# A spectral kernel that also compares its DFT matrices: a smaller table for the comparison, turned on the chip for the second half, and another order of the steps

## The chip, the cores and the metric

The kernel runs on one core of a Trainium2 chip. The metric is device time in microseconds (us), the median of several runs. A profile is one more execution, recorded by the hardware profiler. The engines are TensorE (PE: matmuls, PEld: their weight loads), VectorE (DVE), ScalarE (ACT), GpSimd (POOL) and SyncE (SP). Each works through its own queue in order; semaphores tie them together. Transfers (DMA) are issued by SP and POOL and share 16 DMA engines.

## The reference

Two independent results stand side by side, 2048 rows by 512 columns each, in float32:

```python
# A: global filter
X = jnp.fft.rfft2(x); X = X * (w_r + 1j * w_i); y = jnp.fft.irfft2(X, s=(S, D))
# B: Fourier mixing with given matrices
a = einsum("bsd,ed->bse", x, dft_hid_re); b = einsum("bsd,ed->bse", x, dft_hid_im)
y = einsum("ts,bse->bte", dft_seq_re, a) - einsum("ts,bse->bte", dft_seq_im, b)
```

B's matrices are inputs: two of 2048 x 2048 (`dft_seq`, 16 MB each, called C or `cm` in the kernel) and two of 512 x 512 (`dft_hid`, 1 MB each, `wd`).

## The kernel before

Both halves are computed as fast transforms from tables that are part of the program. For B this is right only if the given matrices are the DFT matrices, so the kernel also loads all of C and `dft_hid` and compares every element with a table. If one differs, a flag is set and a general path (`_b_from_c`, a branch at the end) computes B from the matrices. With the usual inputs that branch is not taken.

**The order is written by hand.** Each piece of work is a named step (`@step`), and the string `PLAN` (line 23) lists all steps; each engine's queue takes its instructions in that order. The names:

- A forward: `xa` loads, `fold` (VectorE), `hid` (TensorE), `zs` (ScalarE), `f16_` (TensorE), `ys` (ScalarE), for eight blocks.
- A per slot n = 0 to 7 of the spectrum: `w` (load of the weights and, right behind, of the slot's table `fi`), `tr` (TensorE), `ez`, `tf` (ScalarE), `sf` (VectorE), `fwd` (TensorE), `wf` (ScalarE), `prod` and `comb` (VectorE, the product with the weights), `yf` (ScalarE), `inv` (TensorE), `ev` (ScalarE).
- A inverse: `hi` (TensorE), `eu` (ScalarE), `g16_` (TensorE), `sc` (ScalarE), `eo` (VectorE), `st` (store by POOL). `hi` and `g16_` use three banks of PSUM in turn with the other steps; `eo` frees a bank.
- B: `xb` loads, `xr` (ScalarE), `al` (TensorE), `av` (ScalarE), `bh` (TensorE), `hv` (ScalarE), `ro` (TensorE), `y1`, `y3` (ScalarE), `y2` (VectorE), `pt` (stores by POOL). `al`, `bh` and `ro` share two banks of PSUM, which `av`, `hv`, `y1` and `y2` free.
- The comparison: `cl` loads 1 MB of C or `dft_hid` into one of six blocks (`blk`, which `xa` and `xb` use too), `cc` compares it on VectorE (`unequal`, line 736: one scalar_tensor_tensor that multiplies by a small constant, compares and counts, in place), `tt` loads a table. `rs`, `pf` and `flag` add up the counts.

The rows of the DFT matrices are symmetric, so a table of 1024 rows by 513 columns, for the cosine and the sine, covers C. It is cut into four tables of 512 rows (`tt0`, `tt1` for the first half of the rows, `tt3`, `tt4` for the second), held in two buffers, and `dft_hid` has its own smaller table (`tt2`, called `hs`). A table serves a whole half of the columns after ScalarE has changed the sign of its odd columns (`sg`, line 754).

**Branch hints.** Twelve steps before the end of the plan (line 823) a hint of the branch at the end is given on PE, ACT and DVE.

Of the kernel before, what the change touches and what calls it, by code (L numbers as in the profile page):

```python
# [24 lines left out]
fold5 xb0 xb3 xb2 hid3 ys1 hid2 zs3 cc0 cl3 f16_3 zs2 cc1 cl4 f16_2 ys3 hid5 ys2 xb1 fold7 hid4 zs5 cl5 f16_5
zs4 cl6 cc2 hid6 ys5 w0 xb4 f16_4 hid7 cc3 ys4 zs6 zs7 f16_6 w1 cc4 xr0 f16_7 sg0 w2 cc5 al0 ys6 late ys7 al1
av0 tr0 cc6 av1 tr1 ez0 wf0 al2 ez1 sf0 al3 av2 sf1 tf0 wf1 fwd0 cl7 av3 xb7 tf1 xb6 xb5 tr2 prod0 xb8 wf2
xb10 fwd1 ez2 cl9 cl8 comb0 fwd2 xb11 cc7 yf0 xb9 xb12 inv0 g2 xr1 prod1 w3 sg1 al4 ev0 sx2 al5 w4 av4 tr3
comb1 av5 spec2 al6 ez3 al7 av6 sf3 yf1 tr4 cl11 av7 prod2 xr2 cl12 inv1 xb13 ez4 tf3 al8 xb15 wf3 comb2 ev1
al9 av8 xb14 wf4 fwd3 av9 sf4 yf2 spy cc8 al10 w5 tf4 al11 av10 cc9 tr5 av11 cl10 inv2 ez5 prod3 cl14 xr3 cl13  # L30
wf5 comb3 al12 w6 ev2 al13 av12 al14 cc10 av13 yf3 al15 av14 fwd4 sf5 cl15 av15 cc11 tf5 bh8 prod4 tt2 tr6 hv8
cl16 wf6 inv3 ez6 comb4 bh0 w7 ev3 sf6 fwd5 yf4 hv0 cc12 tf6 ro0 cc13 cl18 tr7 wf7 cl17 y10 fwd6 ez7 y20 prod5
y30 rx bh1 ry cc14 pt0 bh2 hv1 ro1 comb5 hv2 cl21 cl19 inv4 y11 y21 bh3 yf5 ev4 sf7 y31 prod6 ro2 tf7 pt1 hv3
fwd7 y12 y22 bh4 comb6 y32 pt2 inv5 hv4 cc15 yf6 ro3 ev5 inv6 cc16 y13 cl20 tt3 bh5 ev6 y23 cl22 sg2 prod7 ro4
y33 hv5 pt3 y14 bh6 y24 comb7 y34 ro5 hv6 pt4 bh7 y15 y25 yf7 cc17 y35 inv7 hv7 pt5 ro6 ev7 cc18 tt4 ro7 y16
hi0 cc19 cl23 cl24 y17 cc20 hi1 eu0 cc21 hi2 eu1 cc22 cl25 sg3 cl26 cl30 y27 cl27 g16_0 cc23 y37 pt7 g16_1 eu2
cc24 cl28 sc0 hi3 sc1 eo0 cl29 y26 cc25 y36 hi4 eu3 pt6 eo1 cl31 sg4 cc26 st0 g16_2 g16_3 cc27 eu4 cl32 sc2
hi5 sc3 eo2 eo3 cc28 st1 hi6 eu5 cc29 g16_4 cc30 g16_5 eu6 sc4 cc31 cl33 hi7 sc5 eo4 eo5 g16_6 eu7 cc32 st2
# [189 lines left out]
def kernel(  # L228
# [78 lines left out]
    wsp_sb = const("wsp_sb", 8, 2, 2, 2, src=wsp, by=pool)  # L307
    odd = const("odd", 2, src=tabs["odd"], by=pool)
    turn = sp.tile([P, 8], mybir.dt.int32, name="turn")
    pool.dma_start(turn, tabs["turn"])  # L310
# [288 lines left out]
    def _():
        load(fb, tabs["fb"].rearrange("p (k v n) -> p k v n", k=2, v=2))  # L600
# [138 lines left out]
    def compare(i, k, q, mt, half, tb):  # L739
        raw = "c", i  # L740

        def four(name):
            return at[name].rearrange("p (j c) -> p j c", j=4)

        @step(f"cl{i}")
        def _():
            lo = 4 * half + 2 * q
# [1 line left out]
            load(four(raw).rearrange("p (r j) c -> p r j c", r=2), cm[mt, tb, lo : lo + 2].rearrange("r p j c -> p r j c"))

        if half and tb == 0:
            @step(f"sg{k}")
            def _():
                act.mul(at["t", k][:, :, 1::2], at["t", k][:, :, 1::2], -1.0)
# [8 lines left out]
    def compare_hidden(i, h):
        def four():
            return at["c", i].rearrange("p (j c) -> p j c", j=4)

        @step(f"cl{i}")
        def _():
            block(("c", i))
            load(four().rearrange("p (m j) c -> p m j c", m=2),  # L770
                 wd[:, :, 2 * h : 2 * h + 2].rearrange("m p j c -> m p j c").rearrange("m p j c -> p m j c"))

        if h:
            @step("sg2")
            def _():
                for mt in range(2):
                    act.mul(at["hs"][:, :, mt, 1::2], at["hs"][:, :, mt, 1::2], -1.0)

        @step(f"cc{i}")
        def _():  # L780
            for mt in range(2):
# [4 lines left out]
    def table(k, q, mt):  # L786
        @step(f"tt{k}")
        def _():
            t = sp.tile([P, 4, 513], F32, name="tt", bufs=2)
            if q is None:  # L790
                at["hs"] = t.rearrange("p a b -> p (a b)")[:, :1028].rearrange("p (k m f) -> p k m f", k=2, m=2)
                load(at["hs"], tabs["hs"])
            else:
                at["t", k] = t
                load(t, tabs["tt"][mt, q])

    for k, (q, mt) in enumerate(((0, 0), (0, 1), (None, None), (1, 0), (1, 1))):
        table(k, q, mt)
        if q is None:
            for h in range(2):  # L800
                compare_hidden(16 + h, h)
        else:
            for j in range(8):
                half, tb = divmod(j, 4)
                compare(18 * q + 8 * half + 4 * mt + tb, k, q, mt, half, tb)
# [143 lines left out]
```

## Time and profile before

| What | Value |
|---|---|
| runs (3) | median 191.54 us, 190.98 to 191.56 |
| the profiled execution | 191.75 us, span 190.0 us |
| mean granted TensorE clock | 0.975 |
| loads and stores | 66.05 MB, 348 GB/s over the span |
| compares of C, 128x2048, with and without `odd` | 16 at 2349 ns, 16 at 2286 ns |

The span runs from the first to the last instruction; the rest of the execution's time lies around it. "Busy" adds up the instructions of an engine. Rows of the timeline give start, duration, engine, line, operation, written<-read, and in brackets the idle time before, with what ended it.

### The profile page before, as it was taken

How to read it: one execution, taken by the hardware profiler on the slowest of the kernel's cores; microseconds unless marked ns; L12 is line 12 of the kernel's file. 1: busy time of each engine (PE TensorE's matmuls, PEld its weight loads, DVE VectorE, ACT ScalarE, POOL GpSimd, SP SyncE). 2: the span in 40 equal slices, each digit the busy share in tenths (PEclk: the TensorE clock that was granted, in tenths of full speed). 3: DMA queues.
4: the chain of work that ended last, by engine and by line, in shares of the span. 5: the costliest groups of instructions: out<-in, count | busy, mean ns of one | idle time of the engine just before them, and what ended most of it. 6: DMA issues, size and time to landing. Idle time of an engine off the chain costs nothing.

```text
span 190.0 us, 2792 instructions
## 1 busy us (share of the span) xinstructions
PE 171.7 (90%) x1022; PEld 147.6 (78%) x1022; DVE 162.8 (86%) x217; ACT 88.3 (46%) x145; POOL 23.4 (12%) x32
## 2 busy tenths in 40 slices
...
GB/s 187 303 425 407 430 412 399 406 403 403 378 403 398 398 387 404 284 416 400 389 355 345 307 321 154 197 286 411 232 418 414 411 414 422 418 411 292 200 256 12
DMA packets 19668, 66.05 MB, mean 348 GB/s; under 512 B 1792, under 2 KB 2688, under 8 KB 18752
## 3 DMA queue, kind: packets, MB, share of 16 engines
...
q8 instruction: 10, 0.16, 0.3%
q14 instruction: 10, 0.08, 0.1%
...
## 4 chain that ended last, share of the span: by engine, by line
DMA 35%; PE 30%; DVE 25%; issue 4%; ACT 1%; SPq 1%; DVEq 0%
DMA blk<-in_cm 16%; DVE blk L737 15%; DMA blk<-in_xa 14%; PE pa L515 5%; DMA w<-in_wa 4%; PE pa L447 4%; PE pb L643 4%; PE pb L642 4%; DVE work L571 3%; PE pb L668 3%; PE pa L518 2%; PE pa L425 2%; PE pa L451 2%; PE pb L680 2%; PE pb L664 1%
## 5 line engine op out<-in xcount | busy, mean ns | idle before, releaser
L737 DVE SCALAR_TENSOR_TENSOR blk<-blk,tt 128x2048 f32<-128x2048 f32 (+2 forms) x24 | 41.3, 1752 | 2.6 <-DMA blk<-in_cm 2.6
L737 DVE SCALAR_TENSOR_TENSOR blk<-blk,odd,tt 128x2048 f32<-128x2048 f32 x16 | 37.4, 2349 | 6.7 <-DMA blk<-in_cm 6.6
L550 PE MATMUL pa<-ta,fz 128*128 128x256 f32 x128 | 29.6, 389 | 1.0 <-DVE work L571 1.0
L550 PEld LDWEIGHTS pa<-ta,fz 128*128 128x128 f32 x128 | 28.8, 305 | 1.7 <-issue 1.3
L555 ACT COPY work<-pa 128x1024 f32<-128x1024 f32 x8 | 8.1, 1013 | 22.9 <-PE pa L550 12.0
L485 DVE TENSOR_TENSOR work<-pa,w 128x1024 f32<-128x1024 f32 x14 | 16.4, 1216 | 1.1 <-PE pa L447 1.1
L383 ACT COPY fz<-pa 128x1024 f32<-128x1024 f32 x8 | 15.2, 1976 | 4.3 <-PE pa L379 4.3
L347 DVE TENSOR_TENSOR work<-blk 128x1024 f32<-128x1024 f32 (+1 forms) x10 | 10.1, 1009 | 7.0 <-DMA blk<-in_xa 7.0
L379 PE MATMUL pa<-square,work 128*128 128x128 f32 x128 | 15.3, 276 | 0.7 <-ACT work L372 0.7
L372 ACT COPY work<-pa 128x1024 f32<-128x1024 f32 x8 | 8.0, 1019 | 16.5 <-PE pa L368 16.5
L379 PEld LDWEIGHTS pa<-square,work 128*128 128x128 f32 x128 | 14.9, 194 | 0.9 <-ACT work L372 0.9
L562 PEld LDWEIGHTS pa<-square,work 128*128 128x128 f32 x128 | 14.8, 192 | 0.7 <-issue 0.6
L562 PE MATMUL pa<-square,work 128*128 128x128 f32 x128 | 15.0, 276 | 0.3 <-DVE work L571 0.3
L643 PE MATMUL pb<-fb,xr 128*128 128x200 f32 (+1 forms) x64 | 14.7, 311 | 0.0
L642 PE MATMUL pb<-fb,blk 128*128 128x200 f32 (+1 forms) x64 | 14.6, 310 | 0.0
L515 PEld LDWEIGHTS pa<-fi,work 128*128 128x128 f32 x112 | 13.4, 192 | 1.1 <-issue 1.0
L515 PE MATMUL pa<-fi,work 128*128 128x128 f32 x112 | 13.6, 275 | 0.0
L447 PE MATMUL pa<-work,fi 128*128 128x512 f32 x28 | 13.3, 596 | 0.1
L642 PEld LDWEIGHTS pb<-fb,blk 128*128 128x128 f32 x64 | 10.8, 190 | 0.5 <-issue 0.5
L643 PEld LDWEIGHTS pb<-fb,xr 128*128 128x128 f32 x64 | 10.7, 190 | 0.3 <-ACT xr L632 0.3
L367 PE MATMUL pa<-ta,work 128*128 128x256 f32 x32 | 10.6, 417 | 0.0
L522 ACT COPY fz<-pa 128x1024 f32<-128x1024 f32 x8 | 8.1, 1009 | 5.2 <-PE pa L515 5.2
...
## 6 DMA issues: line engine op xcount, KB each, us to landing
...
tt<-tab_tt SPq DMA_DIRECT2D x4, 1026.0 KB, 9.1
...
```

Source lines behind the costliest of these rows:

```text
L347: TT(out=us[:, h, own].rearrange("p c k f -> p c (k f)"), in0=xs(b)[:, own, 0], in1=xs(b)[:, own, 1], op=op)
L367: mm(even, v[:, 0, 1, r], hd0, start=True, stop=False)
L379: mm(y[:, r, c], zs[:, r, 128 * c : 128 * c + 128], f16, start=True, stop=True)
L383: act.copy(fz.rearrange("p c k (n g) -> p g (c k n)", g=16)[:, i::8], flat(at["py", i]))
L447: mm(flat(px[:, h]), ft[:, 0], flat(t[:, h]), start=True, stop=True)
L485: TT(out=m[:, h].rearrange("p i (r q) f -> p i r (q f)", r=2), in0=x2, in1=w2, op=MUL)
L515: mm(pi[:, i, q], lhs[i], it[:, 0], start=True, stop=True)
L550: mm(pu[:, k, h], gz[:, 2 * h + q, 2 * j + k], at["di"][:, h, q], start=q == 0, stop=q == 1)
L562: mm(po[:, k, q // 2, q % 2], u[:, k, q], f16, start=True, stop=True)
L642: mm(bank[:, lo : lo + w], x[:, g, k], fb[:, n // 15, 0, :w], start=True, stop=False)
L643: mm(bank[:, lo : lo + w], xr[:, g, k], fb[:, n // 15, 1, :w], start=False, stop=True)
L737: dve.scalar_tensor_tensor(raw, raw, k, v, op0=MUL, op1=ALU.not_equal, accum_out=stat[:, i : i + 1])
```

## The change

- **Tables.** Only 512 rows by 513 columns remain, for the cosine (`tt0`) and the sine (`tt1`), both held throughout. For rows 512 to 1023 the angle grows by a quarter turn per column: even columns keep their table up to sign, odd columns take the other table. ScalarE makes this exchange in place between the halves (`swa`, `swb`, with a temporary in a buffer of `yb`).
- **`dft_hid`** is compared with every fourth column of the same table, one matrix per load (before: half the rows of both matrices per load, with its own table).
- **Loads.** `fb`, `odd` and `turn` are one load (`mixed`); `wsp` moves from POOL's queue to SP's; `bt` is cut into `bt` and `bm`.
- **The order** of the plan is another one.
- **Hints.** PE and ACT keep theirs twelve steps before the end; DVE's now stands ahead of the last compare, and POOL and SP get one there too.

The diff, cut to its core:

```diff
 PLAN = """
-xa0 ta tt0 xa1 xa2 xa3 xa5 cl0 fb fold0 cl1 hid0 bt xa7 fold1 tt1 we hid1 zs0 cl2 fold3 f16_0 zs1 f16_1 ys0
+xa0 ta xa1 fb xa2 xa3 cl0 tt0 xa5 fold0 cl1 xa7 fold1 hid0 bm bt zs0 hid1 xb0 fold3 f16_0 zs1 wsp f16_1 ys0
...
-    th = _ang(np.outer(np.arange(S // 2), np.arange(513)), S)
-    tt = np.stack([np.cos(th), -np.sin(th)]).reshape(2, 2, 4, 128, 513).transpose(0, 1, 3, 2, 4)
+    th = _ang(np.outer(np.arange(512), np.arange(513)), S)
+    tt = np.stack([np.cos(th), -np.sin(th)]).reshape(2, 4, 128, 513).transpose(0, 2, 1, 3)
...
+    tt = [const(f"tt{mt}", 4, 513) for mt in range(2)]
...
         @step(f"cc{i}")
         def _():
-            for mt in range(2):
-                for n, (lo, hi, v, neg) in enumerate(((0, 257, at["hs"][:, :, mt], False),
-                                                      (257, 512, at["hs"][:, :, mt, 255:0:-1], mt == 1))):
-                    unequal(32 + 4 * h + 2 * mt + n, four()[:, 2 * mt : 2 * mt + 2, lo:hi], v, -TINY if neg else TINY)
+            t, neg = tt[mt], mt
+            for tb in range(4):
+                unequal(32 + 4 * mt + tb, four(i)[:, :, 128 * tb : 128 * tb + 128],
+                        t[:, :, 512:0:-4] if tb % 2 else t[:, :, 0:512:4],
+                        odd[:, neg * (tb % 2) : neg * (tb % 2) + 1] if tb in (1, 2) else (-TINY if neg * (tb % 2) else TINY))
...
+    @step("swa")
+    def _():
+        tmp = at["tmp"] = sp.tile([P, 2, 512], F32, name="yb", bufs=2).rearrange("p a (j c) -> p (a j) c", j=2)
+        act.copy(tmp, tt[0][:, :, 1::2])
+        act.copy(tt[0][:, :, 1::4], tt[1][:, :, 1::4])
+        act.mul(tt[0][:, :, 3::4], tt[1][:, :, 3::4], -1.0)
+        negate(tt[0][:, :, 2::4])
+
+    @step("swb")
+    def _():
+        act.mul(tt[1][:, :, 1::4], at["tmp"][:, :, 0::2], -1.0)
+        act.copy(tt[1][:, :, 3::4], at["tmp"][:, :, 1::2])
+        negate(tt[1][:, :, 2::4])
...
-    for at_step, name in enumerate(plan):
-        if at_step == len(plan) - 12:
+    last = [name for name in plan if name.startswith("cc")][-1]
+    for name in plan:
+        hinted = {plan[-12]: (pe, act), last: (dve, pool, sync)}.get(name)
+        if hinted:
             tc.no_sync_barrier()
-            tc.mark_branch_hint_location("general", hint="LikelyTaken", engines=[e.engine for e in (pe, act, dve)])
+            tc.mark_branch_hint_location("general", hint="LikelyTaken", engines=[e.engine for e in hinted])
```

What the other order is, at three places. First VectorE's queue where A's forward transform ends and the spectrum begins, before (L737 is a compare, L435 and L436 are `sf0` and `sf1`, L485 is `prod0`):

```order
L737 SCALAR_TENSOR_TENSOR blk,stat<-blk,odd,tt 128x2048
L737 SCALAR_TENSOR_TENSOR blk,stat<-blk,tt 128x2048 x2
L737 SCALAR_TENSOR_TENSOR blk,stat<-blk,odd,tt 128x2048 x2
L435 TENSOR_TENSOR work<-pa,work 128x2x256
L436 TENSOR_TENSOR work<-work,pa 128x2x256
L435 TENSOR_TENSOR work<-pa,work 128x2x256
L436 TENSOR_TENSOR work<-work,pa 128x2x256
L485 TENSOR_TENSOR work<-pa,w 128x1024 x2
```

And now (L744, L439, L440 and L489 are the same four):

```order
L744 SCALAR_TENSOR_TENSOR blk,stat<-blk,mixed,tt_105 128x2048
L744 SCALAR_TENSOR_TENSOR blk,stat<-blk,tt_105 128x2048
L744 SCALAR_TENSOR_TENSOR blk,stat<-blk,tt_106 128x2048
L744 SCALAR_TENSOR_TENSOR blk,stat<-blk,mixed,tt_106 128x2048
L439 TENSOR_TENSOR work<-pa,work 128x2x256
L440 TENSOR_TENSOR work<-work,pa 128x2x256
L439 TENSOR_TENSOR work<-pa,work 128x2x256
L440 TENSOR_TENSOR work<-work,pa 128x2x256
L744 SCALAR_TENSOR_TENSOR blk,stat<-blk,mixed,tt_106 128x2048
L489 TENSOR_TENSOR work<-pa,w 128x1024 x2
```

The last compare of this stage, `cc6`, has moved from ahead of `sf0` to behind `sf1`.

Second, ScalarE's queue in the middle of the kernel, where B's first rows come out, before (L429 is `ez`, L477 `wf`, L689 `y10`, L700 `y30`, L711 and L712 `ry`, L673 `hv`):

```order
L440 COPY work<-pa 128x4
L477 COPY w<-we 128x4
L689 COPY yb<-pb 128x2x257
L429 COPY work<-pa 128x512
L700 COPY yb<-yb 128x2x255
L711 COPY yb<-pb 1x257
L712 COPY yb<-yb 1x255
L673 COPY zb<-pb 128x512 x2
```

And now, from `ez6` (L433) on; L526 is `ev4`, L696 `y10`:

```order
L433 COPY work<-pa 128x512
L802 COPY yb<-tt_105 128x1024
L803 COPY tt_105<-tt_106 128x4x128
L804 ACTIVATE tt_105<-tt_106 128x4x128
L785 ACTIVATE tt_105<-tt_105 128x4x128
L526 COPY fz<-pa 128x2x4x128
L696 COPY yb<-pb 128x2x257
L481 COPY w<-we 128x4
```

The four instructions of `swa` (L802 to L785) now stand ahead of `ev4` and `y10`; the three of `swb` stand in the same way between `ry` and the next `hv`, `hv2`.

Third, the end of VectorE's queue, before (L571 is `eo`, L811 `rs`, L819 `flag`):

```order
L737 SCALAR_TENSOR_TENSOR blk,stat<-blk,odd,tt 128x2048
L942 BRANCH_PREFETCH_HINT
L571 TENSOR_TENSOR work<-pa,work 128x2x2x128 x4
L737 SCALAR_TENSOR_TENSOR blk,stat<-blk,tt 128x2048
L811 TENSOR_REDUCE rs<-stat 128x1
L819 TENSOR_SCALAR flag<-pb 128x1
```

And now:

```order
L744 SCALAR_TENSOR_TENSOR blk,stat<-blk,mixed,tt_106 128x2048
L575 TENSOR_TENSOR work<-pa,work 128x2x2x128 x4
L950 BRANCH_PREFETCH_HINT
L744 SCALAR_TENSOR_TENSOR blk,stat<-blk,tt_106 128x2048
L817 TENSOR_REDUCE rs<-stat 128x1
L825 TENSOR_SCALAR flag<-pb 128x1
```

The hint has moved behind the last four additions of `eo`; the compare, the sum and the flag follow it. The queue of loads changes its order too: `xa1`, `xa2`, `xa3` and `cl0` now stand ahead of `tt0`, and `xb2`, `xb3` ahead of `cl6`.

More of the change, by code (lines that the diff above doesn't have):

```diff
@@ L23 @@
 PLAN = """
-xa0 ta tt0 xa1 xa2 xa3 xa5 cl0 fb fold0 cl1 hid0 bt xa7 fold1 tt1 we hid1 zs0 cl2 fold3 f16_0 zs1 f16_1 ys0
[L25 to L38, printed above, removed]
+xa0 ta xa1 fb xa2 xa3 cl0 tt0 xa5 fold0 cl1 xa7 fold1 hid0 bm bt zs0 hid1 xb0 fold3 f16_0 zs1 wsp f16_1 ys0
@@ new lines @@
+cl2 cc0 hid2 ys1 cl3 fold5 hid3 zs2 f16_2 zs3 xb1 f16_3 ys2 cc1 tt1 hid4 ys3 cl4 fold7 hid5 zs4 cl5 xb2 xb3
+f16_4 zs5 we f16_5 ys4 cl6 cc2 hid7 ys5 cc3 w0 hid6 zs7 sg0 f16_7 zs6 f16_6 ys7 late w1 cc4 ys6 tr0 cc5 w2 tr1
+ez0 xr0 tr2 sf0 ez1 al0 tf0 sf1 al1 av0 cc6 tf1 ez2 fwd0 av1 wf0 al2 prod0 al3 av2 wf1 fwd1 xb4 av3 comb0 xb5
+xb7 xb6 wf2 fwd2 w3 yf0 cl7 prod1 xb8 xb11 xb9 xr1 xb10 tr3 cl8 comb1 inv0 g2 xb12 wf3 ez3 cl9 al4 ev0 sx2 al5
+av4 sf3 yf1 w4 spec2 al6 cc7 tf3 inv1 av5 av6 xb15 al7 prod2 ev1 tr4 xb13 xr2 cl10 fwd3 comb2 ez4 av7 sg1 al8
@@ new lines @@
+xb14 sf4 al9 yf2 av8 spy cc8 cl11 tr5 w5 wf4 al10 av9 ez5 tf4 al11 prod3 av10 inv2 cl12 av11 cl14 xr3 comb3 w6
+al12 ev2 cc9 al13 yf3 av12 wf5 fwd4 sf5 av13 cc10 tf5 al14 al15 av14 prod4 inv3 cl13 av15 cl15 cl17 bh8 ev3
+comb4 w7 wf6 bh0 hv8 cc11 yf4 tr6 hv0 inv4 cc12 ez6 cl18 swa ro0 cc13 cl19 ev4 fwd5 sf6 y10 wf7 bh1 y20 tf6
+cc14 y30 rx fwd6 hv1 ry cc15 cl20 cl16 pt0 bh2 prod5 cl21 swb ro1 tr7 hv2 comb5 y11 bh3 ez7 sf7 yf5 hv3 inv5
+y21 tf7 prod6 y31 ro2 ev5 pt1 ro3 y12 comb6 fwd7 y13 y23 yf6 y22 inv6 y33 prod7 y32 pt3 bh4 ev6 comb7 pt2 bh5
@@ L39 @@
+hv4 cc16 yf7 ro4 hv5 inv7 y14 bh6 y24 ev7 cc17 y34 hi0 hv6 pt4 cc18 cl22 ro5 eu0 cc19 cl24 hi1 y15 y25 cl23
+cc20 y35 bh7 pt5 eu1 cc21 cl25 g16_0 cl27 hv7 hi2 cc22 cl28 sc0 sg2 eo0 cl26 hi3 cc23 eu2 cc24 ro6 g16_1 y16
+cc25 cl29 cl32 hi4 eu3 y26 cl30 sc1 y36 eo1 sg3 pt6 cc26 g16_2 st0 g16_3 sc2 cc27 eu4 ro7 sc3 eo2 hi5 cl31 y17
+y27 eo3 y37 pt7 cc28 hi6 eu5 st1 cc29 cl33 g16_4 cc30 g16_5 eu6 sc4 cc31 hi7 sc5 eo4 eo5 g16_6 eu7 cc32 st2
 g16_7 sc6 eo6 sc7 eo7 st30 cc33 st31 rs pf flag
@@ L305, in _ @@
         load(tf, tabs["first"][:, :641])
[L307 to L310, printed above, removed]
+    wsp_sb = const("wsp_sb", 8, 2, 2, 2)
+    @step("wsp")
+    def _():
+        load(wsp_sb, wsp)
     we = const("we", 8, 2, 2)
+    mixed = const("mixed", 810)
+    fb = mixed[:, :800].rearrange("p (k v n) -> p k v n", k=2, v=2)
+    odd, turn = mixed[:, 800:802], mixed[:, 802:].bitcast(mybir.dt.int32)
     warm = bank_a("warm")
```

88 lines of the change are left out of this document (36 added, 52 removed).

## The prediction

> **What bounds the kernel now.** First the page's totals.
>
> ```profile
> span 190.0 us, 2792 instructions
> PE 171.7 (90%) x1022; PEld 147.6 (78%) x1022; DVE 162.8 (86%) x217; ACT 88.3 (46%) x145; POOL 23.4 (12%) x32
> ```
>
> Two engines are nearly full, so shares of the whole decide nothing. The same execution in stretches of 10 us (time, then busy us of PE, PEld, DVE, ACT, POOL, then clock, DMA share, GB/s):
>
> ```profile
> 60.00:70.00 10.00, 10.00 (x79) 9.90 (x78) 9.97 (x14) 8.41 (x19) 0.00 (x0) 1.00 1.04 394
> 110.00:120.00 10.00, 10.00 (x47) 6.84 (x47) 9.56 (x14) 4.88 (x10) 3.16 (x4) 1.00 0.54 210
> 150.00:160.00 10.00, 10.00 (x62) 9.97 (x62) 6.13 (x8) 4.82 (x6) 2.60 (x3) 1.00 1.02 415
> ```
>
> From 60 to 160 us TensorE is full in each of them. The transfers are full at 60 to 70, half idle at 110 to 120, and full again at 150 to 160. Half idle because the six blocks are all taken and the queue waits for a compare to free one, as SyncE's own waits say; and slow at first, by the page's 40 slices of 4.75 us:
>
> ```profile
> SPq L749 <- DVE blk L737: 42.6, 14, 12.2
> GB/s 187 303 425 407 430 412 399 406 403 403 378 403 398 398 387 404 284 416 400 389 355 345 307 321 154 197 286 411 232 418 414 411 414 422 418 411 292 200 256 12
> ```
>  The timelines (start, duration, in brackets the idle time before and what ended it) show who waits: VectorE first, then TensorE.
>
> ```profile
> 11.01 0.69 DVE L347 TENSOR_TENSOR work<-blk 128x512 f32<-128x512 f32 x1 [3.37 <-DMA blk<-in_xa]
> 49.08 2.35 DVE L737 SCALAR_TENSOR_TENSOR blk<-blk,odd,tt 128x2048 f32<-128x2048 f32 x1 [1.53 <-DMA blk<-in_cm]
> 51.35 0.69 DVE L435 TENSOR_TENSOR work<-pa,work 128x512 f32<-128x512 f32 x1
> 54.91 2.36 DVE L485 TENSOR_TENSOR work<-pa,w 128x1024 f32<-128x1024 f32 x2 [1.08 <-PE pa L447]
> 160.31 2.35 DVE L737 SCALAR_TENSOR_TENSOR blk<-blk,odd,tt 128x2048 f32<-128x2048 f32 x1 [4.18 <-DMA blk<-in_cm]
> 181.09 2.28 DVE L737 SCALAR_TENSOR_TENSOR blk<-blk,tt 128x2048 f32<-128x2048 f32 x1
> 184.14 0.16 DVE L819 TENSOR_SCALAR flag<-pb 128x1 int32<-128x1 f32 x1 [0.53 <-PE pb L815]
> ```
>
> ```profile
> 12.28 0.49 PE L363 MATMUL pa<-ta,work 128*128 128x128 f32 x2 [3.01 <-DVE work L352]
> 52.89 1.98 PE L447 MATMUL pa<-work,fi 128*128 128x512 f32 x4
> 62.54 0.50 PE L642 MATMUL pb<-fb,blk 128*128 128x200 f32 x2
> 63.71 0.50 PE L642 MATMUL pb<-fb,blk 128*128 128x200 f32 x2
> 102.62 0.67 PE L664 MATMUL pb<-bt,yall 128*128 128x257 f32 x2 [0.37 <-DVE yb L695]
> 164.02 3.86 PE L550 MATMUL pa<-ta,fz 128*128 128x256 f32 x16 [1.02 <-DVE work L571]
> 175.38 3.81 PE L562 MATMUL pa<-square,work 128*128 128x128 f32 x32 [0.31 <-DVE work L571]
> ```
>
> Up to about 50 us both engines wait for bytes. From 52.89 us, the first spectrum product fwd0, TensorE waits visibly only 0.37 + 1.02 + 0.31 = 1.70 us. Its last matmuls release eo7; cc33 follows on VectorE at 181.09, then the flag at 184.14. So the end is TensorE's work after fwd0, plus a tail.
>
> **Part by part.** I sum against the profiled execution, 191.75 us (span 190.0, and 1.75 around it), which is 0.21 above the runs' median of 191.54; gains are taken off the median.
>
> *Bytes.* These loads change (KB each, us to landing):
>
> ```profile
> tt<-tab_tt SPq DMA_DIRECT2D x4, 1026.0 KB, 9.1
> tt<-tab_hs SPq DMA_DIRECT2D x1, 514.0 KB, 4.8
> ```
>
> Two tables and the hidden one go: 2 x 1026 + 514 = 2566 KB, 2.63 MB, 6.3 us at the 415 GB/s above. All three were issued after 90 us, so the early stage, which is short of bytes, gets none of it. The small loads that merge are 5 KB together, and wsp only changes queue: nothing, hidden behind folds.
>
> *The first folds.* xa1 is now ahead of tt0's 1026 KB, so fold1 and hid1 start some 2.5 us earlier (1026 KB at 415 GB/s). I take that at zero for the end: up to the table of the first product, both orders hold 17,341 KB. Before: ta 320.5, two tt 2052, fb 400, bt 1475.5, all of xa 4096, seven blocks of C 7168, four xb 1024, w and fi 640, GpSimd's small ones 165. Now fb is 405, bm and bt 704.5 + 771, wsp 32, GpSimd's 128. That table ends the wait, as the next part shows.
>
> *The first product.* Two rows of ScalarE show what fwd0 waited for:
>
> ```profile
> 50.66 0.20 ACT L477 COPY w<-we 128x4 f32<-128x4 f32 x1 [0.37 <-DMA w<-in_wa]
> 52.67 0.17 ACT L440 COPY work<-pa 128x4 f32<-128x4 f32 x1 [0.53 <-DVE work L436]
> ```
>
> w0 had landed at about 50.6, and its table of 128 KB 0.3 us later; the last thing was tf0 at 52.67, behind sf0, which stood behind cc6 on VectorE, and cc6 waited for bytes until 49.08. Now sf0 and sf1 stand ahead of cc6. What is late next is the table: fwd0 at 51.0, not 52.89. From there TensorE's own durations, from the chain (and 63.71 - 62.54 = 1.17 for one group of B):
>
> ```profile
> 54.87 0.87 PE pa L425 x8
> 55.74 1.72 PE pa L447 x4
> 57.46 3.45 PE pa L451 x16
> 60.92 1.78 PE pa L515 x16
> ```
>
> After fwd0 the new order does fwd0 1.72, al2 and al3 2 x 1.17, fwd1 1.72, fwd2 3.45, tr3 0.87, inv0 1.78: 11.9, so 62.9. Before, inv0 was done at 62.54 without tr3; the same work now stands at 62.0. **Gain 0.5 us**: al2 and al3 were done in the wait before, and now come after it. Bounds: 0, and 1.9 if fwd0's whole lead stayed.
>
> *TensorE's waits after that.* The work is the same. The 4.18 us for cc25's load go, since tt3 and tt4 (5 us of transfer) no longer stand ahead of it; with them the 1.02 behind it on TensorE. What is late next there is eo0, eo1 and eo3, which free the banks for the second pass, among compares of 2.3 us. So I credit half of the 1.70, **0.85 us**; bounds 0 and 1.70. VectorE has room: from 54.91 to 184.30 it worked 129.4 less 4.18 and less some 2 us of small waits, 123 us; started at 52.7 (fwd0's end) it could be done at 176.
>
> *The compares of B_dft_hid.* Eight instructions of 512 elements replace eight of 514 and 510; they read the table at every fourth element (every fourth downwards for half of them), four of them with odd:
>
> ```profile
> L737 DVE SCALAR_TENSOR_TENSOR blk<-blk,tt 128x514 f32<-128x514 f32 x4 | 2.8, 688 | 0.0
> L372 ACT COPY work<-pa 128x1024 f32<-128x1024 f32 x8 | 8.0, 1019 | 16.5 <-PE pa L368 16.5
> L383 ACT COPY fz<-pa 128x1024 f32<-128x1024 f32 x8 | 15.2, 1976 | 4.3 <-PE pa L379 4.3
> L754 ACT ACTIVATE tt<-tt 128x1024 f32<-128x1024 f32 x4 | 4.7, 1180 | 0.0
> ```
>
> No row has VectorE reading at such a step. ScalarE writing at every 16th element took 1976 ns where contiguous writes took 1019; at every second one (reading and writing) 1180. Bounds: 0, and 8 x 0.61 = 4.9 us if the time doubles. I take 0, as a read at the step of 2 cost a sixth at most. [...]
>
> *The exchange of odd columns.* ScalarE gets swa (one copy of 1024 elements, three of 512) and swb (three of 512), and loses two of 256 elements. By L754 that is 1.18 + 3 x 0.59 = 2.9, and 1.8 us; doubled at the step of 4, 4.7 and 3.5. ScalarE is 49% busy there, so it has the time. But it works in order: behind swa wait ev4, y10 and, on VectorE, y20 with cc14 behind it; behind swb wait hv2 and y11. swb itself waits for cc15. Zero for the end, as TensorE has fwd5 and bh1 to do meanwhile (1.72 + 2.4).
>
> *The hints.* The tail after the flag:
>
> ```profile
> L942 DVEq BRANCH_PREFETCH_HINT  x1: 51/51/51, 174.5 to 174.5; - x1
> L942 ACTq BRANCH_PREFETCH_HINT  x1: 45/45/45, 175.5 to 175.5; - x1
> L831 DVEq COMPARE_BRANCH  x1: 84/84/84, 185.0 to 185.0; - x1
> L831 ACTq EVENT_SEMAPHORE  x1: 17/17/17, 185.3 to 185.3; - x1
> L831 DVEq EVENT_SEMAPHORE  x1: 21/21/21, 189.0 to 189.0; - x1
> L942 POOLq DRAIN  x3: 45/97/2409, 185.4 to 189.7; - x3
> ```
>
> ScalarE goes on 0.3 us after its branch, VectorE 4.0 us after, though both had a hint ten us ahead. Everyone then waits for VectorE. The next to be late is GpSimd's drain, 185.4 + 2.4 = 187.8. If the hint right ahead of cc33 serves VectorE's branch, 189.0 becomes 187.8: **1.15 us**; if not, 0. I take the gain, as the nearest case, ScalarE's, has a hint that serves, and cc33's start is 3.9 us ahead of the branch (181.09 to 185.0), about the 4.0 to be hidden. [...]
>
> Sum: 0.5 + 0.85 + 1.15 = 2.5; 191.54 - 2.5 = 189.0.
>
> **The rivals.** (a) *The hint changes nothing* (chance 0.26): 189.0 + 1.15 = 190.2. For it: the old hint did nothing either.
>
> (b) *The step of four doubles the compares* (0.15): VectorE, with cc16 to cc22 ahead of eo0, reaches the eo steps 4.9 us later than otherwise, and TensorE's banks come free late. Its 8 us of room shrink to 3, of which waits for eo's banks take the rest: cc33 ends where it did. 191.5, or 190.4 with the hint. [...]
>
> (c) *ScalarE's exchange becomes the path* (0.12), slower: the 512-element pieces cost double (4.7 + 3.5 against 2.9 + 1.8), y20 waits behind swa, so cc14, cc15, and with them swb, come late, and TensorE stands at bh3, whose bank hv2 frees. It decides once hv2 comes more than rx, fwd6, bh2, ro1 and tr7 (0.4 + 1.7 + 2.4 + 0.9 + 0.9 = 6.3 us) after bh1. With no cover left, 1.8 + 1.7 = 3.5 us come on top: 192.5. Against it: ScalarE's 4.88 of 10 busy.
>
> (d) *The bytes count in full* (0.05): 191.54 - 6.3 = 185.2. Against it: the transfers' share of 0.54 at 110 to 120.
>
> **The numbers.** My forecast of 189.0 has the remaining 0.42. A measurement tells some 0.3% from no change, 0.57 us: faster is below 190.97. Faster: 0.42, 0.20 of (a), 0.05 of (b), and (d): 0.72. Same: the rest of (a) and 0.08 of (b): 0.14. Slower: (c) and 0.02 of (b): 0.14. Range: low end with the waits gone wholly (1.70), the hint (1.15), 0.5, and 1.4 for an early stage that fills faster with the table no longer third in the queue (303 raised to 425 GB/s in the second slice, 4.75 x 122 / 425): 186.8; high end (b) without the hint plus half the spread of the runs (0.3): 191.8. It leaves out (c) and (d), 0.17.
>
> **What would show it.** Right: TensorE starts fwd0 near 51.0; no wait of VectorE for a load after 140 us; TensorE's waits after fwd0 under 1 us; VectorE's event after its branch within 3 us. Wrong: pieces of 512 near 1.2 us on VectorE; VectorE at y20 or TensorE at bh3 waiting over 2 us for ScalarE; fwd0 after 52.

## The result, and the profile after

The changed kernel takes 189.89 us in the median of 4 runs (189.51 to 190.4), the kernel before 191.55 beside it: a ratio of 0.9928, 95% interval 0.9909 to 0.9946. A later group of runs gave 190.23 against 190.97, 0.9960 (0.9935 to 0.9986). So it is faster by 0.4 to 0.7 per cent, 0.7 to 1.7 us. The forecast was 189.0 in a range of 186.8 to 191.8. Medians here and below take every execution; ratios leave out a single execution more than 1.5% above the fastest of its kernel, which five of the kernels below have. The profiled execution took 189.85 us, span 188.0.

The page's totals of the changed kernel, and its groups of the hidden compares by form (count, then us in total and mean ns):

```profile
span 188.0 us, 2777 instructions
...
PE 171.4 (91%) x1022; PEld 148.4 (79%) x1022; DVE 166.4 (88%) x217; ACT 93.7 (50%) x150; POOL 24.8 (13%) x29
```

```profile
L744 DVE SCALAR_TENSOR_TENSOR blk<-blk,mixed,tt 128x512 f32<-128x512 f32 x4 | 4.6, 1200 | 0.0
L744 DVE SCALAR_TENSOR_TENSOR blk<-blk,tt 128x512 f32<-128x512 f32 x4 | 4.5, 1133 | 0.0
```

VectorE has 3.6 us more to do than before (166.4 against 162.8): the eight pieces that read every fourth column cost 1133 and 1200 ns where those of 514 elements cost 688. ScalarE has 5.4 us more. Yet the end comes earlier. TensorE's timeline of the changed kernel says where:

```profile
43.50 4.51 PE L429 MATMUL pa<-square,fz 128*128 128x128 f32 x24 [2.04 <-ACT fz L387]
50.55 1.96 PE L451 MATMUL pa<-work,fi 128*128 128x512 f32 x4 [0.21 <-DMA fi<-tab_fi]
62.51 0.51 PE L649 MATMUL pb<-mixed,blk 128*128 128x200 f32 x2
109.77 0.70 PE L671 MATMUL pb<-bt,yall 128*128 128x257 f32 x2 [1.10 <-ACT zb L680]
173.38 3.73 PE L566 MATMUL pa<-square,work 128*128 128x128 f32 x32
```

The first product fwd0 (L451) starts at 50.55, not 52.89, and its table ends the wait. inv0 is done at 62.51 as before, but tr3 (0.87) is now already done by then. The waits of before (0.37 at a bh, 1.02 and 0.31 for eo) are gone; a new one of 1.10 us stands at bh3 (L671), for ScalarE. The last pair of products starts at 173.38, before at 175.38: 2.0 us, which is the whole difference of the spans.

VectorE and ScalarE of the changed kernel, at the exchange and at the end:

```profile
100.93 0.75 DVE L702 TENSOR_TENSOR yb<-yb,pb 128x255 f32<-128x255 f32 x2 [1.55 <-ACT yb L696]
155.06 2.29 DVE L744 SCALAR_TENSOR_TENSOR blk<-blk,tt 128x2048 f32<-128x2048 f32 x1 [0.23 <-DMA blk<-in_cm]
177.81 1.29 DVE L575 TENSOR_TENSOR work<-pa,work 128x512 f32<-128x512 f32 x2 [0.23 <-ACT work L570]
182.22 0.16 DVE L825 TENSOR_SCALAR flag<-pb 128x1 int32<-128x1 f32 x1 [0.68 <-PE pb L821]
```

```profile
97.33 1.16 ACT L804 ACTIVATE tt<-tt 128x512 f32<-128x512 f32 x1
106.19 1.17 ACT L809 ACTIVATE tt<-yb 128x512 f32<-128x512 f32 x1 [2.63 <-DVE blk L744]
109.10 0.61 ACT L680 COPY zb<-pb 128x512 f32<-128x512 f32 x1
```

The exchange's pieces of 512 elements cost 1.13 to 1.18 us each, as much as 1024 at every second column (1.16, L802). y20 (L702) waits 1.55 us for ScalarE, and hv2 (L680 at 109.10) comes behind swb. The wait of 4.18 us for a load at 160 has shrunk to 0.23 us at 155. The tail, in the branch's and the last steps' rows:

```profile
L839 PEldq COMPARE_BRANCH  x1: 489/489/489, 183.0 to 183.0; - x1
L839 DVEq COMPARE_BRANCH  x1: 84/84/84, 183.0 to 183.0; - x1
L839 DVEq EVENT_SEMAPHORE  x1: 21/21/21, 187.0 to 187.0; - x1
```

VectorE's event comes 4.0 us behind its branch, as in the kernel before: the moved hint gained nothing.

### The profile page after: what moved, and what is told of

Read it like the earlier page. It is cut to its first block, busy times and chain, and to the rows that moved or that the text cites. A ratio compares the mean times of both kernels' runs of the same rounds, so it can differ in the third digit from the quotient of the medians.

```text
span 188.0 us, 2777 instructions
## 1 busy us (share of the span) xinstructions
PE 171.4 (91%) x1022; PEld 148.4 (79%) x1022; DVE 166.4 (88%) x217; ACT 93.7 (50%) x150; POOL 24.8 (13%) x29
## 4 chain that ended last, share of the span: by engine, by line
PE 60%; DMA 26%; ACT 5%; DVE 4%; issue 1%; SPq 0%; DVEq 0%; ACTq 0%
PE pa L554 15%; DMA blk<-in_cm 9%; DMA fi<-tab_fi 8%; PE pa L566 8%; DMA blk<-in_xb 7%; PE pa L519 6%; PE pa L451 5%; PE pb L649 4%; PE pb L650 4%; PE pb L675 4%; DVE blk L744 4%; PE pb L687 3%; DMA ta<-tab_first 3%; PE pa L522 2%; PE pa L429 2%; PE pa L455 2%
## 5 line engine op out<-in xcount | busy, mean ns | idle before, releaser
L744 DVE SCALAR_TENSOR_TENSOR blk<-blk,tt 128x2048 f32<-128x2048 f32 (+1 forms) x20 | 40.9, 2062 | 4.7 <-DMA blk<-in_cm 3.9
L744 DVE SCALAR_TENSOR_TENSOR blk<-blk,mixed,tt 128x2048 f32<-128x2048 f32 (+1 forms) x20 | 42.1, 2124 | 1.5 <-DMA blk<-in_cm 1.5
L489 DVE TENSOR_TENSOR work<-pa,w 128x1024 f32<-128x1024 f32 x14 | 16.4, 1215 | 1.3 <-issue 1.0
L387 ACT COPY fz<-pa 128x1024 f32<-128x1024 f32 x8 | 15.1, 1961 | 2.5 <-PE pa L383 2.5
L649 PE MATMUL pb<-mixed,blk 128*128 128x200 f32 (+1 forms) x64 | 14.6, 309 | 0.0
L650 PE MATMUL pb<-mixed,xr 128*128 128x200 f32 (+1 forms) x64 | 14.6, 309 | 0.0
L519 PEld LDWEIGHTS pa<-fi,work 128*128 128x128 f32 x112 | 13.2, 192 | 1.3 <-ACT work L500 0.8
L519 PE MATMUL pa<-fi,work 128*128 128x128 f32 x112 | 13.7, 276 | 0.0
L451 PE MATMUL pa<-work,fi 128*128 128x512 f32 x28 | 13.3, 599 | 0.2 <-DMA fi<-tab_fi 0.2
L649 PEld LDWEIGHTS pb<-mixed,blk 128*128 128x128 f32 x64 | 10.9, 190 | 1.4 <-issue 1.2
L729 POOL DMA_INDIRECT out_b<-yb,mixed x6 | 11.4, 1892 | 1.8 <-issue 1.8
L429 PE MATMUL pa<-square,fz 128*128 128x128 f32 x64 | 9.7, 310 | 2.0 <-ACT fz L387 2.0
L654 ACT COPY yall<-pb 128x344 f32<-128x344 f32 x16 | 7.1, 446 | 8.4 <-PE pb L650 8.2
```

The source lines that it names most:

```text
L387: act.copy(fz.rearrange("p c k (n g) -> p g (c k n)", g=16)[:, i::8], flat(at["py", i]))
L429: pe.transpose(pz[:, r, c], fz[:, c, 2 * e + r], eye)
L451: mm(flat(px[:, h]), ft[:, 0], flat(t[:, h]), start=True, stop=True)
L489: TT(out=m[:, h].rearrange("p i (r q) f -> p i r (q f)", r=2), in0=x2, in1=w2, op=MUL)
L519: mm(pi[:, i, q], lhs[i], it[:, 0], start=True, stop=True)
L649: mm(bank[:, lo : lo + w], x[:, g, k], fb[:, n // 15, 0, :w], start=True, stop=False)
```

## Experiments

All kernels are the changed kernel with the edit shown, unless said otherwise. Each group of runs has the kernel before beside it; ratios are against that.

**The changed kernel once more.** 

> The changed kernel itself, unaltered, beside the other kernels of this group, so that they can be compared with it and not with the kernel before alone. 189.9 us, 0.993 of the kernel before.

190.23 us, 0.9960 (0.9935 to 0.9986); profiled 189.93. It is the reference for what follows. Differences of less than 0.4 us between medians are not read as anything.

**cc6 put back ahead of sf0.**

```diff
-ez0 xr0 tr2 sf0 ez1 al0 tf0 sf1 al1 av0 cc6 tf1
+ez0 xr0 tr2 cc6 sf0 ez1 al0 tf0 sf1 al1 av0 tf1
```

> The changed kernel with the compare cc6 put back ahead of sf0 on VectorE, as in the kernel before. The prediction's step: sf0 stands 2.35 us later, the first product fwd0 follows it to near 52.5 us and the time is 0.5 to 2 us longer (190.4 to 191.9). Rival F (the table fi lands at 50.55 and gates fwd0 anyway): sf0 ends at 50.5 instead of 48.1, fwd0 starts near 50.9 and the time stays at 189.9 within 0.4 us.

193.5 us, 1.0122 (1.0092 to 1.0153): 3.3 us longer than the changed kernel, more than either theory gave. VectorE, ScalarE and TensorE in this kernel, and four stretches of it, of which the third is a part of the second (time, busy us of PE, PEld, DVE, ACT, POOL, then granted clock, DMA share, GB/s):

```profile
48.71 2.35 DVE L744 SCALAR_TENSOR_TENSOR blk<-blk,mixed,tt 128x2048 f32<-128x2048 f32 x1 [1.78 <-DMA blk<-in_cm]
...
52.30 0.17 ACT L444 COPY work<-pa 128x4 f32<-128x4 f32 x1 [4.70 <-DVE work L440]
...
52.52 3.08 PE L451 MATMUL pa<-work,fi 128*128 128x512 f32 x4 [3.08 <-ACT work L444]
```

```profile
49.00:52.50 3.50, 0.43 (x4) 0.22 (x2) 3.50 (x5) 0.20 (x2) 0.00 (x0) 1.00 1.06 393
52.50:56.70 4.20, 4.18 (x8) 2.47 (x9) 1.97 (x3) 1.83 (x5) 0.00 (x0) 0.59 0.76 284
53.50:56.50 3.00, 3.00 (x7) 1.78 (x6) 0.81 (x1) 1.51 (x4) 0.00 (x0) 0.50 0.72 265
56.70:60.00 3.30, 3.30 (x17) 2.43 (x17) 3.23 (x5) 1.09 (x4) 0.00 (x0) 1.00 0.21 37
```

cc6 waits for its load until 48.71, sf0 and tf0 follow, and fwd0 starts at 52.52. That is the prediction's step, to the tenth. What it did not see: in this order al0 and al1 are done by 49.4, so TensorE stands idle for 3.08 us. Soon after it goes on, its granted clock halves: 0.50 from 53.5 to 56.5 us, 0.59 in the mean of the 4.2 us from 52.5. The four matmuls of fwd0 take 3.08 us instead of 1.96, the next group of B is slow as well. fwd0 starts 1.97 us later, takes 1.12 more, and the next group of B 0.65 more (55.39 to 57.20, against 52.35 to 53.51): 3.7 us. TensorE keeps this delay up to its last pair but one (169.92, against 166.18 in the changed kernel), and the last pair then waits 0.70 us for eo. This profile is the longest of the kernel's six executions, 194.67 us, and its span is 4.9 us longer than the changed kernel's; how the 3.3 us of the medians divide between the wait and the clock is not shown.

**swb behind hv2 on ScalarE**, then **swa behind y10 as well**.

```diff
-cc14 y30 rx fwd6 hv1 ry cc15 cl20 cl16 pt0 bh2 prod5 cl21 swb ro1 tr7 hv2 comb5 y11 bh3
+cc14 y30 rx fwd6 hv1 ry cc15 cl20 cl16 pt0 bh2 prod5 cl21 ro1 tr7 hv2 swb comb5 y11 bh3
```

> The changed kernel with the second half of the exchange (swb) moved behind hv2 on ScalarE, nothing else. In the changed kernel ScalarE's hv2 stands behind swb, swb waits 2.63 us for VectorE's compare cc15, and TensorE waits 1.10 us for hv2 at bh3. Theory T (TensorE's row sets the end, VectorE has room): the wait at bh3 goes, the last pair of products starts about 1.1 us earlier than 173.4 and the time is about 188.8 us. Rival V (VectorE, which runs from 101 to 182 us with less than 0.5 us of idle time, sets the end as much): TensorE gains 1.1 us in the middle, gives it back as a wait for VectorE further on, and the time stays at 189.9 within 0.3.

> The changed kernel with swb behind hv2 and also swa behind y10 on ScalarE (its scratch tile is taken where it was, so the buffers rotate as they did). It takes VectorE's wait of 1.55 us at y20 away as well as TensorE's 1.10 us at bh3. Theory T: the time is that of the kernel with swb alone moved, about 188.8 us. Rival V: only this one gains, since both rows move: about 1.1 us, 188.8, against 189.9 with swb alone. If the loads of C bound VectorE behind 150 us, the 1.55 us come back as a wait for a load near 155 us, where it waits 0.23 us now.

Neither gained: 190.58 us, 0.9982 (0.9963 to 1.0001), and 191.41 us, 1.0036 (1.0010 to 1.0061). TensorE with swb behind hv2:

```profile
111.30 2.05 PE L519 MATMUL pa<-fi,work 128*128 128x128 f32 x16 [0.60 <-ACT work L500]
117.73 2.05 PE L519 MATMUL pa<-fi,work 128*128 128x128 f32 x16 [0.94 <-ACT work L500]
```

and VectorE with both moved:

```profile
99.33 0.74 DVE L702 TENSOR_TENSOR yb<-yb,pb 128x255 f32<-128x255 f32 x2
112.23 0.69 DVE L439 TENSOR_TENSOR work<-pa,work 128x512 f32<-128x512 f32 x1 [2.75 <-ACT work L433]
```

The wait at bh3 went, and with both moved the one at y20 too, as both theories said. With swb alone moved, inv5 (L519 at 111.30) waits 0.60 us for yf5, which now stands behind swb on ScalarE, and inv6 (at 117.73) waits 0.94 us for yf6. yf6 (L500) itself waits for VectorE, whose comb6 makes what it reads:

```profile
117.48 0.20 ACT L500 COPY work<-work 128x2 f32<-128x2 f32 x1 [1.75 <-DVE work L495]
```

VectorE still has its wait at y20 in this kernel (1.57 us), so comb6 is no earlier than in the changed kernel, and inv6, there at 117.53, is not either. So theory T falls: the 1.10 us that TensorE waits at bh3 are not by themselves what the exchange costs. V had the mechanism for this kernel, as TensorE's gain comes back as a wait for VectorE. Its time for the second kernel, 188.8, is a miss: VectorE passes y20 1.6 us earlier, but then waits 2.75 us at sf7 (L439) for ez7, which stands behind swb, and TensorE waits 0.54 us at inv5 and 0.94 at inv6 again, and 0.55 at fwd6.

**The exchange in ScalarE's gaps.** swa goes behind ry, where ScalarE waited 2.63 us, swb behind y15, where it waited 4.03. The scratch tile becomes xr's, so that y11 does not need it back; place and tile change together here.

```diff
-        tmp = at["tmp"] = sp.tile([P, 2, 512], F32, name="yb", bufs=2).rearrange("p a (j c) -> p (a j) c", j=2)
+        tmp = at["tmp"] = sp.tile([P, 4, 256], F32, name="xr")
...
-comb4 w7 wf6 bh0 hv8 cc11 yf4 tr6 hv0 inv4 cc12 ez6 cl18 swa ro0
+comb4 w7 wf6 bh0 hv8 cc11 yf4 tr6 hv0 inv4 cc12 ez6 cl18 ro0
...
-cc14 y30 rx fwd6 hv1 ry cc15 cl20 cl16 pt0 bh2 prod5 cl21 swb ro1
+cc14 y30 rx fwd6 hv1 ry swa cc15 cl20 cl16 pt0 bh2 prod5 cl21 ro1
...
-hi1 y15 y25 cl23
+hi1 y15 swb y25 cl23
```

> The changed kernel with the exchange put where ScalarE has long gaps: swa behind ry, in the gap of 2.63 us ahead of hv2 and what hv2 waits behind it, swb behind y15, in the gap of 4.03 us near 134 us; its scratch tile is xr's, which is free by then. Theory T2 (what the first two moves showed: a block of 3 or 4.6 us on ScalarE delays whatever stands behind it, hv2 and bh3 or ez7, sf7, yf5 and inv5; TensorE's wait is moved, not removed): with no work behind the blocks TensorE's waits at bh3 and inv5 (1.10 to 1.54 us in sum) and VectorE's at y20 (1.55 us) all go, and the time falls by about 1.1 us, to 188.8. Rival L (from 135 us on the transfers of C run at 95 to 99 per cent of the DMA engines' time and hold both): the waits go, VectorE waits for loads near 155 us 1 us longer instead, and the time stays at 189.9 within 0.4.

189.51 us, 0.9912 (0.9886 to 0.9938), by the ratios 0.9 us below the changed kernel beside it; the profiled execution's span is 186.9 us, 188.0 in the changed kernel's first profile. One stretch of that profile, then the same of this one:

```profile
101.00:135.00 34.00, 32.90 (x154) 24.19 (x154) 33.79 (x51) 18.23 (x34) 10.84 (x11) 1.00 0.61 222
```

```profile
101.00:135.00 34.00, 34.00 (x162) 25.74 (x161) 33.79 (x51) 21.04 (x36) 9.36 (x11) 1.00 0.64 241
```

inv6 in the changed kernel, then in this one, and this one's TensorE and VectorE near the end:

```profile
117.53 2.05 PE L519 MATMUL pa<-fi,work 128*128 128x128 f32 x16
...
116.14 1.95 PE L519 MATMUL pa<-fi,work 128*128 128x128 f32 x16
...
171.89 3.73 PE L566 MATMUL pa<-square,work 128*128 128x128 f32 x32
...
180.73 0.16 DVE L825 TENSOR_SCALAR flag<-pb 128x1 int32<-128x1 f32 x1 [0.68 <-PE pb L821]
```

TensorE is full in that stretch, its last pair starts at 171.89 instead of 173.38, and the flag comes at 180.73 instead of 182.22. T2 holds in its outcome: in ScalarE's gaps the exchange leaves no wait at y20, bh3 or inv5. What the two kernels above lacked is here: with no wait at y20 and none in its place, VectorE reaches comb6 1.6 us earlier, and inv6 starts 1.4 us earlier, which is nearly all of the 1.5 us at the last pair. Rival L, that the loads take it back, did not show: VectorE waits for no load near 155 us there.

**The hidden compares from neighbouring columns.** ScalarE copies every fourth column of both tables once, where it waits anyway.

```diff
+            act.copy(u[:, mt], tt[mt][:, :, 0:513:4])
...
-                        t[:, :, 512:0:-4] if tb % 2 else t[:, :, 0:512:4],
+                        u[:, :, 128:0:-1] if tb % 2 else u[:, :, :128],
```

> The changed kernel with every fourth column of the two tables copied once by ScalarE into a tile of neighbours (two copies of 516 elements, put where ScalarE waits 2.63 us ahead of swb), and the eight hidden compares reading that tile. Step theory: VectorE's pieces of 512 cost 1.13 to 1.20 us because the read steps by 16 bytes; they fall to about 0.69 us, as in the kernel before, and VectorE's row is 3.6 us shorter. If it is not the step but the pieces themselves, they stay at 1.1 to 1.2 us. On the end: VectorE's last compare cc33 stands behind eo7, which waits for TensorE's last product, so even 3.6 us of room give no more than the 0.23 us that eo7 does not wait: 189.9 within 0.3 us by T. By V, up to 0.5 us where VectorE held TensorE up.

189.99 us, 0.9945 (0.9925 to 0.9965). VectorE's pieces by form, and, from its timeline, a wait that is new:

```profile
L744 DVE SCALAR_TENSOR_TENSOR blk<-blk,mixed,xr 128x512 f32<-128x512 f32 x4 | 2.8, 745 | 0.0
L744 DVE SCALAR_TENSOR_TENSOR blk<-blk,xr 128x512 f32<-128x512 f32 x4 | 2.7, 683 | 0.0
```

```profile
152.88 1.29 DVE L575 TENSOR_TENSOR work<-pa,work 128x512 f32<-128x512 f32 x2 [2.00 <-ACT work L570]
```

The step was the cause: 683 and 745 ns instead of 1133 and 1200. VectorE's busy time falls by 2.9 us, and about as much comes back as waits at the eo steps (2.00, 0.53, 0.50 and 0.17 us) for ScalarE's copies of products that TensorE has only just made. TensorE's wait at bh3 stays at 1.12 us, so ScalarE's extra copies do not hide a gain. The time stays.

**The same, with cc33 ahead of eo6.**

```diff
-g16_7 sc6 eo6 sc7 eo7 st30 cc33 st31 rs pf flag
+g16_7 sc6 cc33 eo6 sc7 eo7 st30 st31 rs pf flag
```

> The kernel with the copied columns, and cc33 moved ahead of eo6 on VectorE. Now the 3.6 us of VectorE's row stand where they can reach the end: cc33's 2.3 us run while TensorE makes the last products, and the flag follows eo7. If the 16-byte-step read costs VectorE 3.6 us, VectorE is free for cc33 near 173 us, eo7 ends near 179.1 as now, the flag comes near 180 instead of 182.2 and the time is about 187.7 us. If VectorE has no such room, eo7 and the last store move back by cc33's 2.3 us and the time is 189.9 or more.

190.11 us, 0.9950 (0.9929 to 0.9971): a miss. The end in its timeline, and the rows of the branch and of the last drains:

```profile
180.85 0.16 DVE L833 TENSOR_SCALAR flag<-pb 128x1 int32<-128x1 f32 x1 [0.68 <-PE pb L829]
...
180.37 0.75 POOL L583 DMA_DIRECT2D out_a<-work  x1 [0.44 <-DVE rs L825]
```

```profile
L847 DVEq COMPARE_BRANCH  x1: 84/84/84, 182.0 to 182.0; - x1
L847 DVEq EVENT_SEMAPHORE  x1: 21/21/21, 186.9 to 186.9; - x1
...
L958 POOLq DRAIN  x3: 39/107/4037, 182.5 to 187.6; - x3
```

The flag does come 1.4 us earlier. But VectorE's event now takes 4.9 us behind the branch, not 4.0, and the last store is issued 1 us later (180.37 against 179.40); GpSimd's longest drain takes 4.04 us, not 2.18, and lasts to 186.5. VectorE's event at 186.9 is the later of the two, about 1.0 us ahead of the end of the span, as in the changed kernel (187.0 of 188.0); with the drain at 186.5 little of the 1.4 us would be left even without it, by an estimate from these rows. Why VectorE's gap grew is open.

**The hints.** No hints at all; then, in the kernel with the exchange in the gaps, VectorE's hint ahead of its last instruction (with w0 ahead of cl6), far ahead of the branch, and no hint but TensorE's.

```diff
-        hinted = {plan[-12]: (pe, act), last: (dve, pool, sync)}.get(name)
+        hinted = {plan[-12]: (pe, act), last: (pool, sync), "flag": (dve,)}.get(name)
```

> The changed kernel without any branch hint. Theory H (a hint spares its engine the fetch of the code behind the branch, and VectorE's alone is not served): ScalarE, TensorE, GpSimd and SyncE, whose first event behind the branch comes 0.5 to 0.9 us after it now, come about 4 us after it like VectorE, and the time stays within 0.5 us, since the latest of them, VectorE, is no later. Rival N (the hints do nothing for any engine; VectorE's 4.0 us are something else): every engine's time behind the branch stays as it is. Rival P (VectorE's hint does part of the work): VectorE's 4.0 us grow, and the time with them.

> The kernel with the exchange in ScalarE's gaps, with two further moves. First, w0 (the loads of the first slot's weights and of its table fi, which lands at 50.4 us and gates fwd0) ahead of cl6 in SyncE's queue: fi lands some 2.5 us earlier, fwd0 then follows ScalarE's and TensorE's own work and starts near 49.7 instead of 50.6; cc6's load comes 1.6 us later and VectorE may wait 1 us for it. If fi is the gate, the time is 0.5 to 0.9 us less than the kernel with the gaps alone; if VectorE's compares are, it is the same or 0.5 more. Second, VectorE's hint is put ahead of its very last instruction, about 1 us ahead of the branch. Theory E (the hinted code is fetched and then lost by the fetches that follow on): the gap of 4.0 to 4.3 us behind VectorE's branch falls to 3 us or less. Rival S (a hint is not served on VectorE at all): the gap stays at 3.6 to 4.3 us.

> The kernel with the exchange in ScalarE's gaps, with VectorE's hint far ahead of the branch, in front of cc28, some 20 us earlier. If the fetch only needs more time, VectorE's gap behind the branch falls from 4.3 us to below 1 us and the time by up to 2 us (the last store's landing and the drains bound it). If a hint isn't served on VectorE, the gap stays at 3.6 to 4.3 us and the time at that of the kernel with the gaps, 189.5.

> The kernel with the exchange in ScalarE's gaps, with TensorE's hint alone and no hint for the other four engines. What the hints' runs showed: TensorE's branch takes 0.49 us with a hint and 3.58 without, VectorE's first event comes 4.0 us behind its branch with a hint wherever the hint stands, and 3.6 without; VectorE's is the last event in all of them. If VectorE's hint costs it 0.4 us, its event comes 3.6 us behind the branch again and the time is 0.4 us below the gaps' 188.9 to 189.5, that is 188.5 to 189.1. If the last store's landing or the drains set the end instead, nothing changes.

Without hints 190.08 us, 0.9944 (0.9924 to 0.9964), not told apart from the changed kernel; the other three 189.36, 0.9918 (0.9885 to 0.9951), 188.88, 0.9883 (0.9861 to 0.9904), and 188.73, 0.9871 (0.9848 to 0.9894). The branch's rows without hints:

```profile
L836 ACTq COMPARE_BRANCH  x1: 50/50/50, 182.9 to 182.9; - x1
L836 PEldq COMPARE_BRANCH  x1: 3582/3582/3582, 183.0 to 183.0; - x1
L836 DVEq COMPARE_BRANCH  x1: 72/72/72, 183.0 to 183.0; - x1
L836 ACTq EVENT_SEMAPHORE  x1: 17/17/17, 183.3 to 183.3; - x1
L836 DVEq EVENT_SEMAPHORE  x1: 21/21/21, 186.6 to 186.6; - x1
```

with the hint 1.7 us ahead of the branch:

```profile
L950 DVEq BRANCH_PREFETCH_HINT  x1: 56/56/56, 179.9 to 179.9; - x1
L839 DVEq EVENT_SEMAPHORE  x1: 21/21/21, 185.6 to 185.6; - x1
```

and 23 us ahead:

```profile
L950 DVEq BRANCH_PREFETCH_HINT  x1: 56/56/56, 158.9 to 158.9; - x1
L839 DVEq EVENT_SEMAPHORE  x1: 21/21/21, 185.8 to 185.8; - x1
```

TensorE's branch takes 3.58 us without a hint and 0.49 with: its hint is served. ScalarE goes on 0.4 to 0.5 us after its branch with or without one, so it never needed it. VectorE's event comes 4.0 us behind its branch in both kernels above (branch at 181.6 and 181.8), 4.0 to 4.9 us in the others with a hint, and 3.6 us without any. Without VectorE's hint but with TensorE's it is 4.2 (181.7 to 185.9), so the expected saving of 0.4 is not there either, and 188.73 against 188.88 is no difference. Theory H's outcome came for TensorE alone: without hints SyncE's first event comes 0.5 us behind its branch, GpSimd's drain 0.2. That a fetch is what TensorE's hint spares is not shown. S holds for VectorE, whose hint gained nothing at any place. What VectorE does in its 4 us is not shown. As its event is the last in all of them (without hints TensorE's, 186.6, comes with it), no hint moves the end.

w0 ahead of cl6 made fwd0 start at 50.05 without a wait. But cc6 then waited 1.14 us for its load, prod0 behind it, and inv0 0.32 us for that: nothing gained (last pair at 171.95).

**The saved bytes put back.** Five loads of 512 KB (2.62 MB) that nobody reads, one into xr, four into a scratch tensor in HBM.

```diff
+                load(scratch[k - 1].rearrange("(p a) d -> p a d", a=2), tabs["tt"][0][:, :2, :512])
```

> The changed kernel with five loads of 512 KB that nobody reads (2.62 MB, what the change saves) put back into SyncE's queue about where the kernel before loads its further tables: one behind prod4, the others behind cc16, cc17, cc18 and cc19. The prediction took the bytes at zero. Theory Z (the transfers have room, VectorE's load wait of 4.18 us in the kernel before was hidden): VectorE waits longer for loads, near 155 us, but the time stays at 190.2 within 0.4. Rival B (from 135 us on the DMA engines are 95 to 99 per cent busy, and VectorE has no idle time left to give): at the 410 GB/s of that stretch the loads take 6.4 us, of which those that fall behind 130 us delay VectorE's compares: 2 to 5 us longer, 192 to 195.

190.68 us, 0.9978 (0.9953 to 1.0002), against 190.23 and 0.9960 for the changed kernel in another group: 0.45 us by the medians, 0.3 by the ratios. The profiled execution took 191.6 us, 0.9 above the median. VectorE in this kernel, then the stretch where most of the loads run:

```profile
102.31 0.75 DVE L702 TENSOR_TENSOR yb<-yb,pb 128x255 f32<-128x255 f32 x2 [2.57 <-ACT yb L696]
156.74 2.29 DVE L744 SCALAR_TENSOR_TENSOR blk<-blk,tt 128x2048 f32<-128x2048 f32 x1 [0.52 <-DMA blk<-in_cm]
183.69 0.16 DVE L833 TENSOR_SCALAR flag<-pb 128x1 int32<-128x1 f32 x1 [0.68 <-PE pb L829]
```

```profile
101.00:130.00 29.00, 27.88 (x133) 19.11 (x132) 27.48 (x42) 17.02 (x33) 9.15 (x9) 1.00 0.81 314
```

From y20 to the flag it takes 81.38 us; the changed kernel takes 182.22 - 100.93 = 81.29. The bytes fill the DMA engines' idle time between 101 and 130 us (share 0.81, 0.57 in the changed kernel). This profile is 1.4 us late at y20, and was as late before the first extra load was issued at 88.7 us: TensorE starts inv at 88.44, in the changed kernel at 87.06, after a wait for B's rows at 82. Theory Z holds, at the edge of its 0.4 us, and B, with 2 us or more, does not. But the loads do not stand quite where the old ones did. Four of the five are issued by 110 us and, but for the first, wait for no buffer; the kernel before issued its two big tables at 120.07 and 132.33 us, and there SyncE's queue stood 9.8 us at the second one for a compare to free the table's buffer, with loads of C behind it. So the run shows that 2.6 MB fit into the idle time of the transfers, not what the tables cost at their old place.

## Why the prediction was right, and where not

- **The first product.** Right in mechanism, and confirmed by undoing it: fwd0 was held by cc6's load through sf0 and tf0, and the table is late next. 50.55 was measured where 51.0 was forecast; the gain by inv0 is 0.9 us (tr3's 0.87 and 0.03), not 0.5. What the step lacked is what its failure would cost in the new order: 3.3 us, as al2 and al3 no longer fill the wait, and in the profile of that kernel the clock falls too, to 0.50 for 3.0 us.
- **TensorE's waits.** Half of the 1.70 was credited. The 1.70 went whole, and 1.10 us appeared at bh3: 0.60 net. With the 0.9, 1.5 of the 2.0 us by which the last pair is earlier has a place; the other 0.5 lies in pauses too short for the rows and is not settled.
- **The bytes.** Zero, as forecast, as far as the run with the bytes put back can tell; rival (d), 6.3 us, is out. With the bytes put back the wait of 4.18 us for cc25's load stays at 0.52, so their amount alone does not bring it back. Whether it was the place of tt3 and tt4 in the queue, as the prediction has it, or the 9.8 us that the queue stood at tt4, no run separates.
- **The hint.** This step failed: "If the hint right ahead of cc33 serves VectorE's branch, 189.0 becomes 187.8". It does not, at any place. The argument went from ScalarE's hint to VectorE's, but ScalarE resumes in 0.4 us without one; the one engine that shows a served hint is TensorE, whose branch (0.49 us, 3.58 without hints) was not quoted. Rival (a)'s 190.2 is what was measured, within the spread of the runs.
- **The compares of B_dft_hid.** The price taken, 0, was wrong: eight pieces at 0.45 and 0.51 us more make 3.8 us, toward the 4.9 of the upper bound. The nearest row was not the step of two but the write at every 16th element, which took 1976 ns against 1019. The step itself is the cost: with the columns copied to neighbours the pieces take 683 and 745 ns, not 1133 and 1200. For the end the 0 stands: rival (b) had the price nearly right and not the effect, as TensorE did not wait for VectorE behind these compares, and when 2.9 us of them were taken away VectorE waited for TensorE's products instead.
- **The exchange.** This zero was wrong too. Rival (c) had the place (y20 behind swa, bh3's bank behind hv2 behind swb) and the doubled price of the pieces, but its 3.5 us at bh3 were 1.10, as fwd6, bh2, ro1 and tr7 covered the rest, and bh3 by itself is not what counted: with that wait alone removed nothing was gained. VectorE, late by its wait at y20, held TensorE at the next join, inv6, through comb6; the prediction named y20, but not this way to the end. The cost is 0.9 us by the ratios and 1.1 us of span, as the kernel with the exchange in the gaps shows, and the other gains outweighed it. The four kernels with the exchange in the gaps lie at 0.9871 to 0.9918 of the kernel before; the lowest, with TensorE's hint alone, takes 188.73 us.

Of the signs set down beforehand, fwd0 came near 51.0. VectorE's event came 4.0 us behind its branch, not within 3; TensorE's waits after fwd0 were 1.10 us, just over 1; and the pieces of 1.2 us came, which were to show the forecast wrong. So the total is right partly by luck: the hint's 1.15 us never came, the waits gave 0.60 for 0.85, and 0.9 for 0.5 ahead of inv0 and the 0.5 us that has no place made good for most of it.
